# Scores in longer runs from tile 10, one transpose moved to a DMA, five stores moved to ScalarE's queue, and new latencies for the planner

## The chip, the cores and the metric

The kernel runs on one core of one Trainium2 chip. The metric is the device time of one execution in microseconds; of several executions the median is taken. A profile of one execution gives the times of single instructions, counted from the start of its span.

## The reference

Attention with a window, followed by a two-layer network on every token:

```python
B, H, S, D = 4, 8, 768, 64                  # q, k, v
keep = (pos_k < 8) | (0 <= pos_q - pos_k < 96)
bias = -slope[h] * dist                     # dist = |q - k|, and 96 for global keys outside the window
a    = softmax(where(keep, q @ k.T / 8 + bias, -1e9))
x    = (a @ v) as (3072 tokens, 512)        # heads side by side
h    = x @ w_in                             # 512 x 2048
out  = (h - tanh(h)) @ w_out                # 2048 x 512, float32
```

## The kernel before

**Tiles.** The 3072 tokens are 24 tiles of 128 rows, six per batch. Tiles are worked in the order `SEQ`: first the four tiles that begin a batch (numbers 0 to 3 below), then the other twenty in order (4 to 23). "Tile 10" here is always a place in that order. Since the window is shorter than a tile, a tile needs the keys of itself (block 0) and of the tile before it (block 1). The 8 global keys are copied into the first places of the previous tile's keys (`a_K`) and values (`a_V`).

**One tile's way.** POOL issues the loads of k, q and v, which cast to bf16 on their way (L237, L243; tiles 0 and 1 load k and q plainly from SP and ACT). k and q are transposed, for tiles 0 to 5 on TensorE (L278, L282, copied out of PSUM in L297), from `PE_T = 6` on by a DMA transpose that SP issues (`a_DT`, L286, into `qk`). The scores of a block (`a_S`, L315) are eight matmuls of 64 rows each, two heads at a time side by side in the array. ScalarE takes the exponential (`a_E`, L324), VectorE multiplies by a mask that holds bias and window (`a_M`, L330), TensorE multiplies by v with a column of ones beside it (`a_AV`, L343 and L347), VectorE divides by the sum (`a_R`, L355 and L356) and leaves `x`. x is transposed, for tiles below `PE_X = 9` on TensorE (`a_X`, L370, copied in L379), else by a DMA transpose on SP's queue (`a_DX`, L382).

**The network.** Tiles 0 to 5 go through it one by one, later ones in pairs. The first matmul (`m1`, L411) gives h in PSUM, with a moving operand of 128 columns for a single tile and 256 for a pair. ScalarE takes tanh (L423), VectorE subtracts (L430) and leaves `g`, the second matmul (`m2`, L445, 512 columns) sums over 16 pieces. The result is copied out of PSUM by ScalarE or VectorE (`m2_e`, L455) and stored (`store`, L460).

**Score runs.** Several blocks' scores can follow each other on TensorE as one run. From tile 4 a run holds the two blocks of one tile; from tile `R3 = 12` on, blocks are put into runs of `RUN = 3`, across tiles. A run holds two of the eight PSUM banks for each of its blocks.

**The order of work.** The program's order is fixed when it is built. `plan()` (from L658) plays the work through with a cost in microseconds for each step, takes at each point the step that can start first, and so writes the order of every engine; on the chip each engine then runs its own list in order, with semaphores between engines. The planner has a small model of DMA: each transfer has an amount of work (`T_ROWS, T_LD, T_W, T_ST, T_DT, T_DX`, L474), queues share the DMA engines by `SHARE`, at some times nothing moves (`FETCHES`, L473), and a transfer's semaphore comes a `TAIL` and a `slack` after its work. A DMA transpose begins, by this model, a fixed time after its issue, longer when loads of POOL are in flight (L713). Scores of a tile are held back until the network's matmuls have come within `AHEAD = 4.5` tiles of it.

**Stores.** `BY_POOL = 21` sends the stores of tiles 0 to 20 through POOL's queue, those of 21 and 22 through ScalarE's, and the three pieces of the last tile through SP's. POOL's queue also issues all loads, the last of them near 136 us.

The lines that the change touches and those that call on them:

Of the kernel before, what the change touches and what calls it, by code (L numbers as in the profile page):

```python
# [15 lines left out]
def kernel(  # L16
# [33 lines left out]
    APART = 4  # L50
    SEQ = [b * NQ for b in range(B)] + [t for t in range(NU) if t % NQ]
    pos = {t: u for u, t in enumerate(SEQ)}
    R3, RUN = 12, 3
    prev_of = {u: pos[t - 1] for u, t in enumerate(SEQ) if t % NQ}
    head_of = {u: pos[t - t % NQ] for u, t in enumerate(SEQ)}
    PLAIN = 2
    PE_T, PE_X = 6, 9
    HT, LAG, NG = 2, 2.0, 4
    SPLIT = (2, 2, 2)
    TJ = 4  # L60
# [400 lines left out]


    AHEAD, AHEAD_T = 4.5, 5.5
    BY_POOL, BY_SP = 21, 0
    YIELD = 0.0
    HALVES = 99
    EB = 2
# [2 lines left out]
    SLACK_DT, SLACK_DX = 1.0, 1.0  # L470
    WARM = (1.1, 7.0)
    COLD = 6.3
    FETCHES = [(15.8, 0.9), (23.0, 0.2), (31.0, 0.3)] + [(a, 0.9) for a in (40, 49, 61, 72, 83, 94, 105, 116, 127, 140)]  # L473
    T_ROWS, T_LD, T_W, T_ST, T_DT, T_DX = 0.67, 0.89, 1.3, 0.65, 1.05, 0.55  # L474
    RING = 5.8
    TAIL = {POOL: 0.45, SP: 0.8, ACT: 0.8}
    SHARE = {
# [180 lines left out]
    def plan():  # L658
# [24 lines left out]
        def fly(jobs, t, t_end):  # L683
            fin = {}
            while t < t_end:
                stop = [(a, n) for a, n in FETCHES if t < a + n][:1] or [(INF, 0)]
                if stop[0][0] <= t:
                    t = min(sum(stop[0]), t_end)
                    continue
                heads = [q for q in jobs if jobs[q] and jobs[q][0][1] <= t]  # L690
                later = min([jobs[q][0][1] for q in jobs if jobs[q] and jobs[q][0][1] > t] + [t_end])
                if not heads:
                    t = later
                    continue
                rate = SHARE[tuple(q in heads for q in (POOL, SP, ACT))]
                rate = {q: r for q, r in zip((POOL, SP, ACT), rate)}
                dt = min([later - t] + [jobs[q][0][2] / rate[q] for q in heads])
                dt = min(dt, stop[0][0] - t)
                t += dt
                for q in heads:  # L700
                    jobs[q][0][2] -= dt * rate[q]
                    if jobs[q][0][2] < 1e-6:
                        key = jobs[q].pop(0)[0]
                        fin[key] = t + TAIL[q] + ops[key]["slack"]
            return fin

        def fly_from(q, key, t, end):
            busy = flying[POOL]
            done.update(fly(flying, at_dma[0], t))
            at_dma[0] = max(at_dma[0], t)  # L710
            begin = end + (2.0 if q is POOL else 1.0)
            if key[0] in ("T", "Xe"):
                begin = t + (4.2 if busy else 2.2)  # L713
            if q is POOL:
                begin = max(begin, RING)
            flying[q].append([key, begin, ops[key]["dma"], q])
            landed[q].append(key)
            done.update(fly({k: [list(j) for j in v] for k, v in flying.items()}, at_dma[0], INF))
# [3 lines left out]
        def due_at(key):  # L722
            if flies[key] or key not in since:
                since[key] = max(
                    [0.0] + [start[a[1]] if a[0] == "issue" else done[a] for a in ops[key]["after"]]
                )
            return since[key]

        def at_of(x):
            return done[x] if isinstance(x, tuple) else x  # L730
# [18 lines left out]
        while ready or any(queues.values()):  # L749
# [16 lines left out]
            for key, n in cand:  # L766
# [4 lines left out]
                t = free[eng]  # L771
                if o["dma"] and len(landed[eng]) >= 8:
                    t = max(t, done[landed[eng][-8]])
                t = max(t, due_at(key))
# [4 lines left out]
                if o["hold"]:  # L779
# [3 lines left out]
                    t = max(t, w)  # L783
                for p in set(o["take"]):
                    n_p = o["take"].count(p)
                    if len(avail[p]) < n_p:
                        t = None
                        break
                    t = max(t, sorted(at_of(x) for x in avail[p])[n_p - 1])
# [7 lines left out]
            _, key, t, eng = best  # L797
# [7 lines left out]
            if o["at"]:  # L805
                done[key] = o["at"]
            elif o["dma"]:
                fly_from(o["eng"], key, t, end)
            else:
                done[key] = end + LAT[o["eng"]]  # L810
# [95 lines left out]
```

## Time and profile before

| what | value |
|---|---|
| median of 6 runs | 212.7 us (212.47 to 212.98) |
| the profiled execution's own time | 212.47 us |
| its span, first to last instruction | 210.7 us |
| granted TensorE clock, mean | 0.997 |
| TensorE's busy time | 205.6 us, 98% of the span |
| VectorE, ScalarE, POOL | 130.5, 118.7, 84.0 us |
| DMA transposes of k and q (18) | issue to landing 3.3 / 5.1 / 8.6 us (least, median, most) |
| DMA transposes of x (15) | 2.4 / 3.4 / 7.7 us |
| stores from POOL (21) | 0.58 us of POOL each, 2.3 to 6.6 us to landing |

A matmul's time in the profile is from its issue to its result, and matmuls follow each other before that, so the mean of one is longer than its share of the engine; the pieces of the chain of work that ended last show what each group took of the engine. The span leaves out what lies before the first and after the last instruction, 1.8 us in this execution.

### The profile page before, as it was taken

How to read it: one execution, taken by the hardware profiler on the slowest of the kernel's cores; microseconds unless marked ns; L12 is line 12 of the kernel's file. 1: busy time of each engine (PE TensorE's matmuls, PEld its weight loads, DVE VectorE, ACT ScalarE, POOL GpSimd, SP SyncE). 2: the span in 40 equal slices, each digit the busy share in tenths (PEclk: the TensorE clock that was granted, in tenths of full speed). 3: DMA queues.
4: the chain of work that ended last, by engine and by line, in shares of the span. 5: the costliest groups of instructions: out<-in, count | busy, mean ns of one | idle time of the engine just before them, and what ended most of it. 6: DMA issues, size and time to landing. Idle time of an engine off the chain costs nothing.

```text
span 210.7 us, 5364 instructions
## 1 busy us (share of the span) xinstructions
PE 205.6 (98%) x2198; PEld 145.2 (69%) x2198; DVE 130.5 (62%) x271; ACT 118.7 (56%) x182; POOL 84.0 (40%) x113
## 2 busy tenths in 40 slices
PE   7899999999999999999999999999999999999993
PEld 2669976876657758656957686668667676666663
DVE  6569865835767878465957595648548494434311
ACT  4767846535575685376648574848466763344420
POOL 8995685619548266466054520910110110111000
PEclk9999999999999999999999999999999999999998
DMA  5999999999999999999989995993510121110012
GB/s 178 185 188 177 189 192 181 189 149 141 248 178 185 160 153 152 136 159 204 129 157 145 124 194 109 112 157 82 123 55 20 60 49 52 53 50 18 37 50 100
DMA packets 104729, 27.49 MB, mean 130 GB/s; under 512 B 94656, under 2 KB 103104, under 8 KB 104704
## 3 DMA queue, kind: packets, MB, share of 16 engines
q0 software_dynamic: 75728, 18.62, 88.2%
q1 hardware_dynamic: 28144, 7.48, 23.9%
q10 hardware_dynamic: 832, 1.05, 1.5%
q8 instruction: 17, 0.28, 0.6%
q14 instruction: 8, 0.07, 0.1%
HBM read 27.26 MB, written 6.29 MB: 159 GB/s over the span
## 4 chain that ended last, share of the span: by engine, by line
PE 95%; DMA 2%; DVE 1%; ACT 0%; issue 0%; DVEq 0%
PE ps L411 41%; PE ps L445 40%; PE ps L315 6%; PE ps L343 3%; PE ps L347 2%; DMA kf<-in_k_dram 2%; PE ps L278 1%; PE ps L370 1%; PE ps L282 1%; PE ps L166 1%; DVE kh L297 0%; ACT qk L297 0%; DVE kq L256 0%; DVE ot L455 0%; DVEq L297 0%
## 5 line engine op out<-in xcount | busy, mean ns | idle before, releaser
L411 PE MATMUL ps<-xT,w_in_bf 128*128 128x256 bf16 (+1 forms) x960 | 96.3, 251 | 0.0
L445 PE MATMUL ps<-w_out_bf,g 128*128 128x512 bf16 (+3 forms) x416 | 93.3, 363 | 0.0
L411 PEld LDWEIGHTS <-w_in_bf 128*128 128x128 bf16 x960 | 77.2, 98 | 16.7
L423 ACT ACTIVATE th<-ps 128x512 f32<-128x512 f32 (+1 forms) x102 | 57.3, 574 | 53.5 <-PE ps L411 52.6
L430 DVE TENSOR_TENSOR g<-ps,th 128x512 bf16<-128x512 f32 (+1 forms) x102 | 64.3, 653 | 36.4 <-ACT th L423 35.8
L445 PEld LDWEIGHTS <-g 128*128 128x128 bf16 x416 | 38.3, 98 | 30.4
L460 POOL DMA_DIRECT2D out_dram<-ot x21 | 11.9, 568 | 90.4 <-ACT ot L455 87.4
L324 ACT ACTIVATE pd<-ps 128x1024 bf16<-128x1024 f32 x24 | 24.6, 1026 | 6.9 <-PE ps L315 6.9
L243 POOL DMA_DIRECT2D kq<-in_k_dram x20 | 18.0, 900 | 14.7 <-DMA qk<-kq 11.0
L324 ACT ACTIVATE po<-ps 128x1024 bf16<-128x1024 f32 x20 | 20.5, 1026 | 4.9 <-PE ps L315 4.9
L237 POOL DMA_DIRECT2D vb<-in_v_dram x24 | 21.8, 910 | 0.1
L455 ACT COPY ot<-ps 128x512 f32<-128x512 f32 x20 | 11.7, 586 | 12.0 <-PE ps L445 12.0
L330 DVE TENSOR_TENSOR po<-po,mk 128x1024 bf16<-128x1024 bf16 x20 | 13.8, 691 | 7.2 <-ACT po L324 7.2
L243 POOL DMA_DIRECT2D kq<-in_q_dram x20 | 18.0, 899 | 0.1
L356 DVE TENSOR_TENSOR x<-ps,rden 128x512 bf16<-128x512 f32 x24 | 16.6, 691 | 0.8
L330 DVE TENSOR_TENSOR pd<-pd,mk 128x1024 bf16<-128x1024 bf16 x20 | 13.8, 689 | 5.1 <-ACT pd L324 5.1
L343 PE MATMUL ps<-vb,pd 128*128 128x65 bf16 x192 | 14.1, 193 | 0.0
L343 PEld LDWEIGHTS <-pd 128*128 128x128 bf16 x192 | 12.5, 98 | 1.1 <-ACT pd L324 0.2
L347 PE MATMUL ps<-vb,po 128*128 128x65 bf16 x160 | 12.4, 193 | 0.0
L315 PEld LDWEIGHTS <-qk 64*128 64x128 bf16 x288 | 8.1, 94 | 5.3 <-issue 5.1
L315 PE MATMUL ps<-qk 64*128 64x128 bf16 x288 | 10.8, 217 | 0.0
L347 PEld LDWEIGHTS <-po 128*128 128x128 bf16 x160 | 10.4, 97 | 0.5
(49 smaller groups left out, 84.7 us busy)
## 6 DMA issues: line engine op xcount, KB each, us to landing
out_dram<-ot POOLq DMA_DIRECT2D x21, 256.0 KB, 3.2
vb<-in_v_dram POOLq DMA_DIRECT2D x24, 128.0 KB, 6.3
kq<-in_k_dram POOLq DMA_DIRECT2D x22, 128.0 KB, 5.9
kq<-in_q_dram POOLq DMA_DIRECT2D x22, 128.0 KB, 6.0
w_in_bf<-in_moe_w_in_dram POOLq DMA_DIRECT2D x8, 256.0 KB, 8.1
w_out_bf<-in_moe_w_out_dram POOLq DMA_DIRECT2D x8, 256.0 KB, 9.3
kf<-in_k_dram SPq DMA_DIRECT2D x2, 256.0 KB, 4.6
qf<-in_q_dram ACTq DMA_DIRECT2D x2, 256.0 KB, 3.9
```

The lines of the kernel that those rows point to most:

```text
L237: i = nc.gpsimd.dma_start(out=v_of(u)[:, :, 0:Dh], in_=by_head)
L243: i = nc.gpsimd.dma_start(out=dst.rearrange("p (h d) -> p h d", d=Dh), in_=by_head)
L315: nc.tensor.matmul(s[:, slot(2 * p + hh), :], kT(prev_of[u] if o else u)[r, p, :], qk[u][r, 0, p, :], start=u >= B, stop=True, skip_group_ ...
L324: nc.scalar.activation(pr[u, o].rearrange("q (a h) f -> q a h f", a=2)[:, part], sc[u, o][:, part, :].rearrange("q a (h f) -> q a h f", f= ...
L330: nc.vector.tensor_tensor(out=pr[u, o], in0=pr[u, o], in1=mk[:, :, mask_of(u, o) - 1, :], op=ALU.mult)
L343: nc.tensor.matmul(dst, pr[u, 0][:, slot(h), :], v_of(u)[:, h, :], start=True, stop=last,)
L347: nc.tensor.matmul(dst, pr[u, 1][:, slot(h), :], v_of(prev_of[u])[:, h, :], start=False, stop=True,)
L356: nc.vector.tensor_tensor(out=xs[u].rearrange("q (a h) d -> q a h d", a=2), in0=t[:, :, :, 0:Dh], in1=rden.to_broadcast([P, 2, H // 2, Dh] ...
L411: nc.tensor.matmul(t[:, (f - f0) * n : (f - f0 + 1) * n], w_in_bf[j][:, c, fo : fo + P], xT[b][:, c, o : o + n], start=(c == 0), stop=(c = ...
L423: nc.scalar.activation(h_view(ths[g, f0], g, m), h_view(hs[g, f0], g, m), AF.Tanh, bias=0.0, scale=1.0)
L430: nc.vector.tensor_tensor(out=gs[b][:, f0 : f0 + m, o : o + n], in0=h_view(hs.pop((g, f0)), g, m), in1=h_view(ths.pop((g, f0)), g, m), op= ...
L445: nc.tensor.matmul(os_[u, part][:, 0 : hi - lo], gs[b][:, f, t * P : (t + 1) * P], w_out_bf[f // FJ][:, f % FJ, lo:hi], start=(f == 0), st ...
```

## The change

Five edits. From tile 10 instead of 12, score blocks go in runs of three. x of tile 8 is transposed by a DMA on SP's queue instead of TensorE, so tile 8 is the first of its kind. Stores of tiles 16 to 20 are issued by ScalarE instead of POOL. In the planner, the times in which no DMA moves are cut (0.9 us to 0.4, and 0.2 and 0.3 to 0.1), three amounts of DMA work are lowered by 0.01 us, and a DMA transpose is taken to begin 3.4 us after its issue instead of 4.2 when loads are in flight, and 2.0 instead of 2.2 when none are. The last three alter no instruction themselves; they alter the order that the planner writes.

```diff
-    R3, RUN = 12, 3
+    R3, RUN = 10, 3
...
-    PE_T, PE_X = 6, 9
+    PE_T, PE_X = 6, 8
...
-    BY_POOL, BY_SP = 21, 0
+    BY_POOL, BY_SP = 16, 0
...
-    FETCHES = [(15.8, 0.9), (23.0, 0.2), (31.0, 0.3)] + [(a, 0.9) for a in (40, 49, 61, 72, 83, 94, 105, 116, 127, 140)]
-    T_ROWS, T_LD, T_W, T_ST, T_DT, T_DX = 0.67, 0.89, 1.3, 0.65, 1.05, 0.55
+    FETCHES = [(15.8, 0.9), (23.0, 0.1), (31.0, 0.1)] + [(a, 0.4) for a in (40, 49, 61, 72, 83, 94, 105, 116, 127, 140)]
+    T_ROWS, T_LD, T_W, T_ST, T_DT, T_DX = 0.66, 0.88, 1.29, 0.65, 1.05, 0.55
...
             if key[0] in ("T", "Xe"):
-                begin = t + (4.2 if busy else 2.2)
+                begin = t + (3.4 if busy else 2.0)
```

## The prediction

> **What bounds the kernel now.** I read the page's head and its fourth part first, then the stretches of 20 us, then the chain piece by piece, and last the stretches around single DMA transposes. The head and the chain:
>
> ```profile
> span 210.7 us, 5364 instructions
> PE 205.6 (98%) x2198; PEld 145.2 (69%) x2198; DVE 130.5 (62%) x271; ACT 118.7 (56%) x182; POOL 84.0 (40%) x113
> PE 95%; DMA 2%; DVE 1%; ACT 0%; issue 0%; DVEq 0%
> ```
>
> TensorE is busy for 98% of the span and makes 95% of the chain. Busy matmuls overlap, so I check this against the stretches (columns: stretch, sum, PE, PEld, DVE, ACT, POOL, clock, DMA share, GB/s):
>
> ```profile
> 20.00:40.00 20.00, 20.00 (x317) 16.67 (x315) 14.52 (x32) 12.30 (x22) 14.83 (x20) 1.00 1.60 191
> 40.00:60.00 20.00, 20.00 (x235) 13.17 (x232) 12.18 (x22) 9.68 (x14) 10.93 (x14) 1.00 1.80 172
> 60.00:80.00 20.00, 20.00 (x235) 13.97 (x230) 15.48 (x31) 14.30 (x20) 9.07 (x11) 1.00 1.82 171
> ```
>
> No idle time, full clock. The chain's pieces show that PE is not only covered but fed: 16 m2 matmuls of 512 columns take 3.45 to 3.56 us, or 216 to 222 ns each, as everywhere else. The waits of PE sum to 1.7 us in the whole run, all before 16 us. So only two things can move the end: the sum of PE's work, and a new wait of PE.
>
> **What the Trainium skill says.** "TensorE: Matmul & The Clock Gate", section "Wait — 56ns, not 53.3ns?", gives 55.6 ns for a warm 128-column matmul; the trace agrees, four transposes take 0.22 us. "DMA: Bandwidth & Descriptors", section "Issuing engines are not separate DMA queues", says that DMAs issued from ScalarE, SyncE and GpSimd share the same 16 engines and interleave, and that another issuer only saves sequencer time. The trace agrees: a store costs 0.54 to 0.60 us on POOL and 0.35 on ACT's queue, and landings stretch under load (the same DMA transpose takes 3.3 to 8.6 us). Section "Queues, rings and completion order" of that page has each engine round-robin between the rows with work; so a transpose issued amid loads waits for packets of loads, which fits that spread.
>
> **The PE sum.** x of tile 8 leaves PE: four transposes.
>
> ```profile
> 64.97 0.55 PE ps L315 x16
> 65.52 0.33 PE ps L370 x4
> 118.35 0.78 PE ps L315 x24
> ```
>
> Elsewhere in the chain the same four take 0.22 us; the 0.33 here has the changeover after a score run in it, which whatever follows pays. So 0.22 to 0.23 us go. The copy behind them (0.58 us on ACT or 0.42 on DVE) goes too, worth nothing, since neither engine holds PE.
>
> The score runs look like a gain and are none. Before: blocks of tiles 4 to 11 in 8 runs of two, tiles 12 to 23 in 8 runs of three, with the first four tiles 20 runs. After, counted in the built program: 6 runs of two, 9 of three, one of a single block, again 20. A run pays about 0.10 us when it begins and 0.095 when it ends (L315's start-to-start steps beside its neighbours); 16 matmuls take 0.55 us and 24 take 0.78, 0.23 per block either way. Zero.
>
> PE's other matmuls are the same number (2198 less 4). Sum: -0.23 us.
>
> **New waits: DMA transposes.** The fitted figures make the planner believe that a transpose lands 0.8 us sooner when loads are in flight and 0.2 sooner otherwise, so it sets the score runs earlier. PE's order is unchanged for the first 370 matmuls (to 28.5 us), SP's and POOL's to 56 us. I take each transpose's margin in the trace and subtract the PE work that the built program no longer puts ahead of its reader. Tile 6 (columns: start, us, what):
>
> ```profile
> 37.54 1.33 SPq L286 DMA_TRANSPOSE qk<-kq  x1
> DMA to landing us min/median/max: 8.3/8.3/8.3
> 47.97 0.62 PE L315 MATMUL ps<-qk 64*128 64x128 bf16 x16
> ```
>
> It lands at 45.9 and is read at 47.97: margin 2.1. In the new order 32 m1 matmuls of 128 columns (56 ns each, 1.8 us) stand behind this run instead of ahead. Left: 0.3 us. Tile 9:
>
> ```profile
> 53.18 1.65 SPq L286 DMA_TRANSPOSE qk<-kq  x1
> DMA to landing us min/median/max: 8.6/8.6/8.6
> 64.90 0.40 PE L315 MATMUL ps<-qk 64*128 64x128 bf16 x8
> ```
>
> Landed 61.8, margin 3.1; 8 m2 (1.73 us) and 8 m1 of 256 columns (0.88) move behind it: 0.5 left. Tile 7: 5.6 - 1.8 = 3.8. Tile 8: 4.6 - 1.7 = 2.9. Tile 11: 5.5 - 2.8 = 2.7. Tile 14: 7.15 - 4.6 = 2.6. x of tiles 12 and 13: 3.5 - 1.7 = 1.8. The rest keep more. Weights: the sixth piece of w_out landed at 39.6, was read at 41.3, and its reader moves up by 1.1: 0.6 left; the seventh and eighth keep over 2.
>
> So with the landings of the trace nothing waits, but the cushion falls from 2.1 us to 0.3 at one place and to 0.5 at another. A wait of PE is lost time in full: PE runs in order and is full up to the end, so the tanh, g and m2 behind it are all late by as much. Once PE has slipped at tile 6 the later margins grow by the slip; delays don't add.
>
> **The other parts.** Tile 8's x on SP: one DMA transpose more, 1.19 us of the queue, 2.4 to 7.7 to landing. x of tile 8 was written at 65.06, and the matmuls that lead to it move up by 1.7, so SP has it from 63.3 and is done with it near 64.5. Behind it on SP stands tile 11's k/q transpose, issued at 64.59 in the trace when its loads had landed: up to 0.6 later (1.2 if x comes late), of the 2.7 us left. Behind that, tile 9's x and tile 12's k/q with 2.7 and 4.8. Its own readers, the m1 of tiles 8 and 9, waited for tile 9's x anyway (landed 75.27, read 79.27, moved up 1.3: 2.7 left). POOL's next loads wait for k/q transposes, so they shift by the same tenths; tile 14 has 2.6 for it. Cost zero; with that cover gone, 1.2 us once.
>
> Runs of three at tiles 10 and 11: six of eight PSUM banks held while three exps follow on ACT (0.92 us apart). Eight such runs in the trace cost PE nothing. Here they fall into the stretch where DVE has 15.5 and ACT 14.3 busy of 20 us, the fullest. Bound: nothing, or one exp (0.92) at each of one or two of the places. I take nothing.
>
> Stores of tiles 16 to 20: five issues of 0.35 us onto ACT, ahead of the next tanh. From 160 us ACT is busy 11.2 and then 8.4 of 20 us, with gaps of about 1.1 us before a tanh; hidden. If all showed, 1.75 us. POOL loses five stores after its last load (137 us), nothing waits for them. The last tile's stores stay on SP, so the tail from the last matmul (207.3) to the end stays about 3.4 us.
>
> **Sum.** The profiled execution took 212.47 with its span of 210.7, 1.8 around it. Less 0.23: span 210.45, time 212.24. The six runs lie in two heaps, 212.47 to 212.53 and 212.87 to 212.98, and the profile is of the lower; the median, 212.7, less 0.23 is 212.47. I say 212.5.
>
> **Rivals.** A measurement of this kernel can tell about 0.2% (0.43 us) from no change.
> 1. No wait, or waits under 0.66 us in sum: 212.3 to 213.1. For it, the margins above, all positive. Chance 0.48.
> 2. Tile 6's or 9's k/q transpose lands late. For it: landings of equal transposes spread from 3.3 to 8.6 us, and the order of stores against loads on POOL changes from 56 us, inside tile 9's flight; against: until 46 us both queues issue the same in the same order. Landing x later than in the trace costs x - 0.3 (tile 6) or x - 0.5 (tile 9); with the 0.23 gained, it is slower by over 0.43 from x of 1 us. x = 1.3: 213.2 to 213.5; x = 2: 214.2. Chance 0.20.
> 3. ACT or DVE falls behind at the runs of three from tile 10: one or two exps, 0.9 to 1.8, so 213.4 to 214.3. Against it, the eight runs without cost. Chance 0.12.
> 4. The stores on ACT show: up to 1.75, 214.2. Chance 0.03.
> 5. Faster by over 0.43: the 0.23 with the upper heap's 0.4 us gone, 212.1. That needs the upper heap to come from a wait that the new order avoids; the profile is of the lower heap and shows none. Chance 0.17.
> That the change does nothing would be 212.7 and lies in case 1.
>
> **Numbers.** Faster 0.17, same 0.48, slower 0.35 (cases 2 to 4). The range leaves out the ends of cases 2 to 4 and 5: 212.0 to 214.2. Case 1's own: 212.3 to 213.1.
>
> **What would show it.** L370 with 32 matmuls instead of 36, SP with 16 x transposes, ACT with seven stores, 20 runs of L315; last matmul near 207.0; PE 20.00 in every stretch of 20 us from 20 to 200. Wrong: a wait of PE on the qk transposes near 46 or 62 us, idle PE between 60 and 80 with ACT or DVE as releaser, a gap before a tanh that follows a store on ACT, or a start before 16 us that is other than before.

## The result, and the profile after

The changed kernel takes 214.01 us (median of 18 executions, 212.4 to 216.9) against 212.62 (39 executions, 212.23 to 213.43) for the kernel before, taken in turn on the same chips. The ratio is 1.0059, with an interval of 1.0042 to 1.0076: slower by 0.6%. The ratios here and below leave out executions marked as slow (here the one of 216.9 us, with a mean clock of 0.992; below, one or two each in three experiments), so a ratio can be smaller than that of the medians beside it. The executions of the changed kernel lie 4.5 us apart, those before 1.2, so the loss is not a fixed amount. The forecast was 212.5 and no measurable change; 214.01 lies in its range of 212.0 to 214.2, but on the side of rivals 2 to 4, not of the case taken as likeliest.

The profiled execution took 214.11 us, 1.64 more than the profiled one of before: its span grew by 1.30 us, and what lies before the first and after the last instruction from 1.78 us to 2.13. The head of the profile's page of the changed kernel, and its chain:

```profile
span 212.0 us, 5354 instructions
PE 205.8 (97%) x2194; PEld 145.0 (68%) x2194; DVE 129.2 (61%) x264; ACT 122.2 (58%) x188; POOL 81.2 (38%) x108
PE 85%; DMA 11%; DVE 1%; ACT 1%; issue 1%; DVEq 0%
PE ps L411 37%; PE ps L445 35%; DMA qk<-kq 9%; PE ps L315 5%; PE ps L343 3%; PE ps L347 2%; DMA kf<-in_k_dram 2%; PE ps L278 1%; PE ps L282 1%; PE ps L370 1%; PE ps L166 1%; DVE kh L297 0%; DVE qk L335 0%; ACT qk L297 0%; ACT po L324 0%
```

TensorE has the 2194 matmuls that were counted and still leads, but DMA went from 2% of the chain to 11%, and 9% of that is one kind: the DMA transposes of k and q. The clock was full throughout this execution. The stretches of 20 us (columns as in the prediction: sum, PE, PEld, DVE, ACT, POOL, clock, DMA share, GB/s):

```profile
20.00:40.00 20.00, 20.00 (x314) 16.55 (x311) 13.88 (x29) 13.37 (x23) 15.15 (x20) 1.00 1.60 191
40.00:60.00 20.00, 18.53 (x230) 12.59 (x229) 13.08 (x24) 9.35 (x15) 7.43 (x11) 1.00 1.90 158
60.00:80.00 20.00, 19.89 (x218) 13.75 (x217) 13.82 (x27) 12.83 (x19) 12.11 (x15) 1.00 2.06 170
```

Before, all three held 20.00 of PE. Now 1.47 us are missing before 60 us. The waits of PE in the changed kernel (us in total, times, longest), and PE's timeline around the gap (start, us, what, and in brackets the idle time before it and what ended it):

```profile
PE ps L315 <- DMA qk<-kq: 1.5, 1, 1.5
```

```profile
56.90 1.03 PE L445 MATMUL ps<-w_out_bf,g 128*128 128x512 bf16 x4
59.39 0.62 PE L315 MATMUL ps<-qk 64*128 64x128 bf16 x16 [1.47 <-DMA qk<-kq]
```

This is the score run of tile 8: k and q of that tile were not yet transposed. A smaller wait of the same kind stands inside the first run of three that tile 11 takes part in. It shows on the queue of weight loads (PEld), since the sixteen weight loads of tile 10 in that run were through and its matmuls had begun:

```profile
75.30 0.23 PEld L315 LDWEIGHTS <-qk 64*128 64x128 bf16 x8 [0.28 <-DMA qk<-kq]
```

The first matmul of the run of tile 8 starts 1.53 us later than the usual changeover would have it; tile 9 loses 0.04 and tile 11 0.27. Sum 1.84; less the 0.23 us of PE work that went, 1.61. The last matmul starts at 208.90 instead of 207.27, 1.63 later. So the whole delay of PE in this execution is late transposes of k and q. (The 0.35 us outside the span are another matter; see the point on the tail at the end.)

How late, and beside what? Tile 8's transpose in the changed kernel, its issue on SP's queue and its way to landing, then the three stores (256 KB each) that POOL issued just after it:

```profile
48.08 1.24 SPq L286 DMA_TRANSPOSE qk<-kq  x1
DMA to landing us min/median/max: 11.3/11.3/11.3
L460 POOL DMA_DIRECT2D out_dram<-ot x3: 562/590/597, 48.4 to 49.5; - x3
DMA to landing us min/median/max: 9.6/9.6/9.7
```

And the same in the kernel before, the transpose first:

```profile
L286 SPq DMA_TRANSPOSE qk<-kq x1: 1233/1233/1233, 48.4 to 48.4; - x1
DMA to landing us min/median/max: 6.6/6.6/6.6
L460 POOL DMA_DIRECT2D out_dram<-ot x3: 545/592/599, 49.4 to 50.6; - x3
DMA to landing us min/median/max: 5.8/6.1/6.2
```

The transpose of the same 256 KB takes 11.3 us instead of 6.6, and the stores 9.6 instead of 6.1. The stores landed between 58.0 and 59.1 us, the transpose at 59.34, right behind them. Tile 7's transpose ahead of it on the queue took 7.1 us instead of 4.4, and in the trace the packets of tile 8's start about when tile 7's have landed: at 52.6 us with a landing at 52.78, before at 51.1 with a landing at 50.76. From that landing on, tile 8's took 6.6 us instead of 4.2. The stretches of 4 us show that the DMA engines moved less. Changed kernel first, then before; the last column is GB/s:

```profile
48.00:52.00 4.00, 4.00 (x60) 3.06 (x58) 3.36 (x8) 1.75 (x3) 2.04 (x4) 1.00 2.33 110
52.00:56.00 4.00, 4.00 (x56) 2.85 (x54) 2.62 (x6) 1.92 (x3) 2.65 (x3) 1.00 1.95 139
56.00:60.00 4.00, 2.53 (x39) 1.70 (x38) 2.49 (x4) 1.86 (x4) 0.16 (x2) 1.00 1.19 224
```

```profile
48.00:52.00 4.00, 4.00 (x45) 2.48 (x45) 2.66 (x5) 1.94 (x2) 3.81 (x6) 1.00 1.78 147
52.00:56.00 4.00, 4.00 (x60) 3.06 (x58) 3.09 (x6) 1.65 (x3) 2.01 (x3) 1.00 1.40 276
56.00:60.00 4.00, 4.00 (x52) 2.19 (x49) 2.27 (x4) 2.56 (x4) 3.22 (x4) 1.00 1.80 137
```

From 48 to 56 us the engines moved 4 x (110 + 139) = 996 KB, before 4 x (147 + 276) = 1692. With a higher busy share (2.33 against 1.78 in the first stretch) they moved less; what was outstanding then came after 56 us, at 224 GB/s. Tile 8's transpose belonged to it.

The shortfall is not even. From 49.5 to 50.5 us hardly anything moved: 3 and 9 GB/s in the two halves. In the experiment below with the stores back on POOL, which has the same order up to there, it is 2 and 9; in the five profiled executions that still have the old order there (the kernel before, the planner's figures undone, and each of the three visible parts alone) it is 138 to 215. A second such stretch lies from 55.5 to 56.5 us, with 35 and 38 GB/s against 285 and 124 before. Both fall into the flight of tile 8's transpose, so by estimate they make some 2 of the 4.7 us by which it is longer. The planner's list has a stop of this kind at 49 us, and the change cut it from 0.9 us to 0.4. What makes the engines stop isn't shown.

### The profile page after: what moved, and what is told of

It reads as the page before. It is cut to its first block, busy times and chain, and to the rows that moved or that the text cites. A ratio compares the mean times of both kernels' runs of the same rounds, so it can differ in the third digit from the quotient of the medians.

```text
span 212.0 us, 5354 instructions
## 1 busy us (share of the span) xinstructions
PE 205.8 (97%) x2194; PEld 145.0 (68%) x2194; DVE 129.2 (61%) x264; ACT 122.2 (58%) x188; POOL 81.2 (38%) x108
## 4 chain that ended last, share of the span: by engine, by line
PE 85%; DMA 11%; DVE 1%; ACT 1%; issue 1%; DVEq 0%
PE ps L411 37%; PE ps L445 35%; DMA qk<-kq 9%; PE ps L315 5%; PE ps L343 3%; PE ps L347 2%; DMA kf<-in_k_dram 2%; PE ps L278 1%; PE ps L282 1%; PE ps L370 1%; PE ps L166 1%; DVE kh L297 0%; DVE qk L335 0%; ACT qk L297 0%; ACT po L324 0%
## 5 line engine op out<-in xcount | busy, mean ns | idle before, releaser
L445 PE MATMUL ps<-w_out_bf,g 128*128 128x512 bf16 (+3 forms) x416 | 94.7, 363 | 0.0
L460 POOL DMA_DIRECT2D out_dram<-ot x16 | 9.2, 582 | 38.4 <-ACT ot L455 38.4
L455 ACT COPY ot<-ps 128x512 f32<-128x512 f32 x19 | 11.1, 585 | 8.8 <-PE ps L445 8.5
```

The source lines that it names most:

```text
L445: nc.tensor.matmul(os_[u, part][:, 0 : hi - lo], gs[b][:, f, t * P : (t + 1) * P], w_out_bf[f // FJ][:, f % FJ, lo:hi], start=(f == 0), st ...
```

## The experiments

The theory after the result: the planner's new figures set the score runs earlier and make loads, stores and transposes fall together in another way; a DMA transpose then lands after its run, and PE stands. Rivals: the runs of three press ScalarE or VectorE, the x transposes in SP's queue push the k/q transposes back, or the stores on ScalarE cost something. The measured ratios are to the kernel before, taken in the same turns.

### The planner's figures undone, the rest kept

```diff
-    FETCHES = [(15.8, 0.9), (23.0, 0.1), (31.0, 0.1)] + [(a, 0.4) for a in ...]
-    T_ROWS, T_LD, T_W, T_ST, T_DT, T_DX = 0.66, 0.88, 1.29, 0.65, 1.05, 0.55
+    FETCHES = [(15.8, 0.9), (23.0, 0.2), (31.0, 0.3)] + [(a, 0.9) for a in ...]
+    T_ROWS, T_LD, T_W, T_ST, T_DT, T_DX = 0.67, 0.89, 1.3, 0.65, 1.05, 0.55
...
-                begin = t + (3.4 if busy else 2.0)
+                begin = t + (4.2 if busy else 2.2)
```

> The changed kernel with all of the planner's figures as they were before (4.2 and 2.2 us to the begin of a DMA transpose, the old stops and amounts of work); runs of three from tile 10, tile 8's x by DMA and the stores on ScalarE's queue stay. Theory 'margins' (the planner's new figures set score runs before their transposes land): score runs of tiles 6 to 9 stand where they stood before, tile 11's 1.5 us later, so no wait on qk; four transposes less on TensorE: 212.3 to 212.6, no slower than before. Theory 'added DMA' (tile 8's x on SP, stores on ScalarE's queue, or runs of three make the waits): waits stay, 213.5 or more.

Measured: 212.74 us, ratio 1.0006 (0.9995 to 1.0017). No score run waits for a DMA. The last matmul starts at 207.05, 0.22 earlier than before (207.27): the sum of PE's work was right. With runs of three from tile 10, x of tile 8 by DMA and the stores on ScalarE all in place, the kernel is as fast as before. These three together cost nothing that can be told when planned with the old figures.

### The planner's figures alone

The edit is the reverse of the last, on the kernel before.

> The kernel before with the planner's new figures alone; x of tile 8 on TensorE, runs of three from tile 12, stores on POOL. Theory 'margins': tiles 6 to 9 move up by 1.7 to 2.6 us as in the changed kernel, tiles 10 and 11 by 4.4, so TensorE waits on qk near 46 to 76 us, with a wide spread: 213.3 to 215. Theory 'added DMA': no wait, 212.6.

Measured: 214.91 us, ratio 1.0076 (1.0044 to 1.0109). PE's timeline of this kernel, where most of the loss is:

```profile
71.76 1.03 PE L445 MATMUL ps<-w_out_bf,g 128*128 128x512 bf16 x4
74.39 0.62 PE L315 MATMUL ps<-qk 64*128 64x128 bf16 x16 [1.60 <-DMA qk<-kq]
```

That is tile 11 (landed 74.34). Tiles 6 and 10 were also read right at their landing and lost 0.16 and 0.19. So the figures alone are enough to make transposes late, and which tile is hit differs from the changed kernel. With the run before, this puts the loss on the planner's figures, and on no instruction that was added or removed.

### The stores back on POOL

```diff
-    BY_POOL, BY_SP = 16, 0
+    BY_POOL, BY_SP = 21, 0
```

> The changed kernel with the stores of tiles 16 to 20 back on POOL; TensorE's order is the same as in the changed kernel. Theory 'margins': same waits, 213.5 to 214.5. Theory 'stores on ScalarE': back at 212.5.

Measured: 214.21 us, ratio 1.0056 (1.0035 to 1.0076), as slow as the changed kernel. TensorE's order is the same as there, and ScalarE issues its first store at 164.9 us there, long after the waits. The waits of this kernel:

```profile
PE ps L315 <- DMA qk<-kq: 0.9, 2, 0.7
```

Here tile 8 landed at 58.16 and lost 0.25, tile 9 lost 0.77 and tile 11 0.15. Up to these places the program does not differ from the changed kernel, where it was 1.53, 0.04 and 0.27. The loss is much the same, but its place moves between executions of one order: a landing is not a fixed number.

### Thin stores: is it the stores' traffic?

In the changed kernel's order, tiles 0 to 7 store only 32 of their 512 columns; the rest of these tiles' output is left out. Nothing else is touched.

```diff
+        if u < 8:
+            hi = lo + 32
```

> The changed kernel in unchanged order, but of tiles 0 to 7 only 32 of 512 output columns are stored: the rest of those rows is left out. If the stores of the first tiles share the DMA engines with the k/q transposes and so make them land late, the transposes of tiles 7 to 9 land about 2 us sooner and the waits near 58 and 64 us go: 212.3 to 213. If the lateness comes from the loads alone, the waits stay: 213.5 to 214.5.

Measured: 212.76 us, ratio 1.0004 (0.9993 to 1.0016). Tile 8's transpose and PE's timeline at its run, in this kernel:

```profile
DMA to landing us min/median/max: 7.1/7.1/7.1
...
57.16 1.03 PE L445 MATMUL ps<-w_out_bf,g 128*128 128x512 bf16 x4
58.12 0.62 PE L315 MATMUL ps<-qk 64*128 64x128 bf16 x16
```

The transpose lands at 55.69, 2.4 us ahead of its reader, and tile 9's takes 4.8 us instead of 10.0. All waits on `qk` are gone with the order unchanged. So it takes the stores' traffic to make the transposes late; their place behind one another in SP's queue and the reader's place are unchanged and don't do it alone. This agrees with what the Trainium skill states in "DMA: Bandwidth & Descriptors", section "Queues, rings and completion order": an engine takes turns between the rows that have work, so a transpose shares with whatever else is outstanding. Whether bytes or the number of packets decide was not tried. Nor is it separated how much the stores do by sharing and how much by the stop near 49.5 us, which is shorter here: 65 and 247 GB/s in the two halves from 49.5 to 50.5.

### Which of the figures

Only the begin of a transpose restored to 4.2 and 2.2:

```diff
-                begin = t + (3.4 if busy else 2.0)
+                begin = t + (4.2 if busy else 2.2)
```

> The changed kernel with only the begin of a DMA transpose back at 4.2 and 2.2 us; the shorter stops stay. In the built order the score runs stand against those of the kernel before: tile 6 up by 1.8 us, tiles 7 to 9 by 0.9 each, tile 11 by 2.0. Theory 'margins': between the two, waits at tiles 6 to 9 in part of the executions, 212.7 to 213.7. Theory 'the begin alone does it': 212.4 to 212.6.

Measured: 213.79 us, ratio 1.0051 (1.0036 to 1.0065). The waits for transposes are gone, with 1.7 us of margin at tile 6, 3.1 at tile 8 and 1.9 at tile 9. But this order has waits of another kind:

```profile
PE ps L315 <- DVE x L356: 1.0, 1, 1.0
...
PE ps L411 <- DVE rden L355: 0.5, 1, 0.5
```

A score run waits for VectorE's divide to free its PSUM. In the profiled execution the loss has another cause, these 1.5 us of waits and a later start (tile 4's run begins at 23.22 instead of 22.79 us). The run says that the shorter begin is needed for the late transposes, not that restoring it is enough.

Only the times in which nothing moves, and the amounts of work, restored (the first four lines of the first diff):

> The changed kernel with only the stops and the amounts of DMA work as before; the begin of a DMA transpose stays at 3.4 and 2.0. Tile 6 where it stood before, tiles 7 and 8 up by 0.9, tile 9 as before. Theory 'margins': hardly a wait, 212.4 to 213.0. Theory 'the begin alone does it': waits stay, 213.5 or more.

Measured: 212.35 us, ratio 0.9988 (0.9976 to 1.0000), with no wait on `qk`; 2.8 us of margin at tile 8 and 2.5 at tile 9, though the begin stays short. So in the profiled executions each half undone takes the late transposes away; it is both together that bring the runs too close. This is the fastest version with all of the visible parts of the change, at the edge of what can be told from no change.

### More slack instead

The planner adds a slack to each transpose of k and q; it goes from 1 us to 4, all else as in the changed kernel:

```diff
-    SLACK_DT, SLACK_DX = 1.0, 1.0
+    SLACK_DT, SLACK_DX = 4.0, 1.0
```

> The changed kernel with 4.0 instead of 1.0 us of slack for the landing of a k/q transpose in the planner, all else as changed. Score runs of tiles 6, 7, 9 and 10 stand 0.8 to 3.5 us later than in the kernel before. Theory 'margins': no wait on qk, spread as narrow as before, 212.2 to 212.6. Theory 'added DMA' (the x transpose and the stores on ScalarE's queue slow landings for good): 213 or more.

Measured: 212.76 us, ratio 1.0001 (0.9985 to 1.0017). Every transpose of k and q lands at least 2 us ahead of its reader. The new figures do no harm once runs keep a distance; two waits for VectorE of 0.2 us each appear, which is about the 0.22 that should have been gained.

### Two x transposes by DMA

On the kernel before, x of tiles 7 and 8 by DMA, with slack of 2 us:

```diff
-    PE_T, PE_X = 6, 9
+    PE_T, PE_X = 6, 7
...
-    SLACK_DT, SLACK_DX = 1.0, 1.0
+    SLACK_DT, SLACK_DX = 2.0, 2.0
```

> A try at a faster version: the kernel before with x of tiles 7 and 8 by DMA and 2.0 us of slack for both kinds of transpose in the planner, all else as before. Eight transposes less on TensorE, 0.45 us. Score runs of tiles 7 to 9 later than before, tile 10 up by 3.1 of a margin of 6.8. Theory 'margins': 212.1 to 212.4. If the added transposes push landings back by more than 3 us: 213 or more.

Measured: 217.24 us, ratio 1.0205 (1.0172 to 1.0238), a miss in size and in cause. The waits of PE, and the stretch in which they lie:

```profile
PE ps L343 <- DVE pd L330: 1.7, 1, 1.7
...
PE ps L411 <- DMA xT<-x: 0.7, 1, 0.7
PE ps L347 <- DVE po L330: 0.7, 1, 0.7
```

```profile
60.00:80.00 20.00, 16.81 (x181) 11.65 (x180) 11.87 (x22) 11.62 (x17) 12.00 (x15) 0.91 1.89 162
```

PE lacks 3.2 us here, and the granted clock is 0.91 in this stretch, where the next four stretches have 1.00; so beside the 3.1 us of waits, PE's work was slower too. The trace's clock record has 0.50 from 70.87 to 74.28 us and 1.00 around it. PE's timeline has it right after the third wait:

```profile
71.16 5.16 PE L411 MATMUL ps<-xT,w_in_bf 128*128 128x256 bf16 x32 [0.74 <-DMA xT<-x]
```

Eight such matmuls take 0.87 us elsewhere (70.89 to 71.76 in the kernel with the planner's figures alone), 32 of them 3.5; here they take 5.2. All six executions of this kernel have a mean clock of 0.992, so it is not a chance of one. That the two x transposes do it by themselves isn't shown, since the order changed with the slack as well.

### One part alone, on the kernel before

Stores of tiles 16 to 20 on ScalarE's queue:

```diff
-    BY_POOL, BY_SP = 21, 0
+    BY_POOL, BY_SP = 16, 0
```

> The kernel before with the stores of tiles 16 to 20 on ScalarE's queue and nothing else; the order of TensorE is that of the kernel before. All theories that put the loss on the planner's figures: 212.5, no difference, no wait of TensorE. If a store on ScalarE's queue holds a tanh up: up to 1.75 us more.

Measured: 212.39 us, ratio 0.9989 (0.9977 to 1.0001). PE's order is that of before and the last matmul starts at the same 207.27, but the span is 210.3 instead of 210.7. The end is shorter. At the end of the program SP waits for the semaphores of the DMAs one by one, in a list whose order is the same in all traces here. SP's waits of this kind by stretches (count, durations in ns, first and last start), and the drain after them, in before:

```profile
L901 SPq EVENT_SEMAPHORE  x2: 28/28/28, 209.4 to 209.5; - x2
...
L901 SPq EVENT_SEMAPHORE  x6: 28/28/28, 209.5 to 209.8; - x6
L901 SPq DRAIN  x2: 7/10/13, 209.9 to 209.9; - x2
```

And in this kernel:

```profile
L901 SPq EVENT_SEMAPHORE  x6: 27/28/28, 208.3 to 208.6; - x6
...
L901 SPq EVENT_SEMAPHORE  x2: 28/28/28, 209.4 to 209.4; - x2
L901 SPq DRAIN  x1: 13/13/13, 209.5 to 209.5; - x1
```

In both, the last store lands at about 209.4. Before, it signals a semaphore (102) that is third in the list, so seven waits of about 0.06 us each follow; with the stores moved, it signals another (117), next to last, two such waits follow, and most of the list has been walked by 208.6. So the five moved DMAs changed which semaphore the last one gets. From the last matmul to the end of the span it is 3.06 us here and 3.42 before, 0.36 less, which the prediction did not have: five waits less make 0.31 of it, and the last store landed 0.05 sooner.

x of tile 8 by DMA, alone:

```diff
-    PE_T, PE_X = 6, 9
+    PE_T, PE_X = 6, 8
```

> The kernel before with x of tile 8 by DMA alone. Theory 'sum of TensorE' (only the four transposes and the landings count; no score run moves up by more than 2.8 us of 7.1): 212.2 to 212.4. Theory 'new list' (every new plan is a new order, and where the planner's costs of VectorE are below the trace's, as 0.61 for a mask product that takes 0.69, TensorE waits on VectorE): 1 to 2 us more, with VectorE as releaser between 60 and 130 us, as in the run with the begin undone.

Measured: 214.05 us, ratio 1.0068 (1.0047 to 1.0089): the sum of TensorE missed, and the theory 'new list' was right in size and in releaser. PE's timeline of this kernel:

```profile
94.05 0.23 PE L315 MATMUL ps<-qk 64*128 64x128 bf16 x1
95.75 0.60 PE L315 MATMUL ps<-qk 64*128 64x128 bf16 x15 [1.47 <-DVE g L430]
```

and VectorE's work just before:

```profile
94.40 0.69 DVE L356 TENSOR_TENSOR x<-ps,rden 128x512 bf16<-128x512 f32 x1
95.01 0.68 DVE L430 TENSOR_TENSOR g<-ps,th 128x512 bf16<-128x512 f32 x1
```

No transpose is late. The new order puts a score run into PSUM that a subtraction of VectorE still reads, and puts a divide ahead of that subtraction. The planner counts a subtraction at about 0.60 us and a mask product at 0.61; the trace has 0.68 and 0.69. That these small errors led the planner to this order is argued; no run with corrected costs was made.

Runs of three from tile 10, alone:

```diff
-    R3, RUN = 12, 3
+    R3, RUN = 10, 3
```

> The kernel before with runs of three from tile 10 alone. Same number of runs, same matmuls. Theory 'sum of TensorE': 212.5. Theory 'new list': 212.6 to 213.2 with VectorE as releaser; theory 'margins' has no wait on qk here, since tiles 6 to 9 stand where they stood and tiles 10 and 11 stand later.

Measured: 212.93 us, ratio 1.0008 (0.9993 to 1.0022); no wait on `qk`, last matmul at 207.34. To within what can be told, the runs of three are the zero that was counted.

### A version with the stops undone and some slack

On the changed kernel: the stops and amounts as before (the same lines as in "Which of the figures"), and a slack of 1.5 us for k/q transposes and 2.0 for those of x.

```diff
-    SLACK_DT, SLACK_DX = 1.0, 1.0
+    SLACK_DT, SLACK_DX = 1.5, 2.0
```

> A try at a faster version: the changed kernel with the stops and amounts of before and, in the planner, 1.5 us of slack for k/q and 2.0 for x transposes. Tiles 6 to 11 stand against the kernel before at 0, up 0.9, and then 0.5 to 4.1 us later; x of tiles 10 and 11 1.8 later. Theory 'margins' with 'new list': no wait on a transpose, at most 0.2 us on VectorE, four transposes less: 212.2 to 212.5, with the spread of the kernel before.

Measured: 213.36 us, ratio 1.0025 (1.0012 to 1.0038), a miss. The waits list only work at the start:

```profile
PE ps L393 <- DVE zero L865: 1.0, 1, 1.0
PE ps L282 <- DMA kq<-in_k_dram: 0.3, 1, 0.3
```

Work also begins later: tile 4's run starts at 23.38 us instead of 22.79, which with the 0.22 us saved puts the last matmul at 207.64. The span ends 4.1 us after it, where the changed kernel and five others with these stores on ScalarE have 3.03 to 3.09 (the planner's figures undone, 3.71, is the second exception). The traces show where: the last store landed 2.57 us after its issue, against 1.51 in the run with more slack, where it was issued at the same 208.28 us; with the planner's figures undone the last two took 2.39 and 2.14. Why these stores took longer is open, and whether the other executions of this kernel did the same isn't on record. No version beats the kernel before by more than can be told.

## Why the prediction was wrong, point by point

**The PE sum, -0.23 us.** Right: 0.22 in the profiled execution where the order is planned with the old figures. The zero for the runs of three held when tried alone.

**Moved readers.** Right as to the order. Tile 8's run was to move up by 1.7 us from 59.58; without its wait it would have begun at 59.39 - 1.53 = 57.86, which is 1.72.

**"With the landings of the trace nothing waits."** This is the step that failed. It took landings from one execution of another order and subtracted only the reader's move. Tile 8 was credited with 2.9 us left; its landing moved from 54.95 to 59.34, by 4.4, so 1.5 were missing: the wait that was measured. Tiles 6 and 9, called the tightest, kept 1.39 and nearly nothing (0.04 lost). The change moves the loads and stores as well as the readers, and the thin stores show that the stores' traffic decides whether the landing comes in time. Part of the 4.4 is the spread of one order: the kernel before, the planner's figures undone and the three visible parts alone have the same order on PE, POOL and SP until after this landing, and there it comes at 54.95, 55.96, 55.95, 56.72 and 57.07. The trace that the margin was taken from has the earliest of the five. The other 2.3 us, from 57.07 to 59.34, lie outside that spread; with the stores back on POOL, a second execution of the new order, it is 58.16, also later than all five. The prediction had the evidence: equal transposes from 3.3 to 8.6 us, and "a transpose issued amid loads waits for packets of loads". A margin of 2.9 us against a spread of 5 us was no margin, and rival 2 held that spread only against the two tightest tiles.

**"SP's and POOL's order is unchanged to 56 us."** Unchanged order did not mean unchanged overlap. Tile 7's transpose was issued at 45.66 instead of 46.36 and the three stores at 48.36 instead of 49.43, so they met other traffic. How much of the stretch from 6.6 to 11.3 us comes from this shift alone was not separated; two stretches of about 1 us in which almost nothing moved lie in it, and in none of the five executions of the old order did the first of them occur.

**Rivals.** Rival 2 is right in kind, with 0.20, and in the size that it gave (213.2 to 214.2), but it named tiles 6 and 9. Rivals 3 and 4 did not act in this kernel; rival 3's mechanism, VectorE late at a score run, shows in two experiments (the begin restored, x alone), though not with runs of three alone.

**"Cost zero" for the stores and the x transpose.** Right for the stores on ScalarE. Of the x transpose alone the run shows a loss of 0.7%, by VectorE in the order that was written for it and not by SP's queue; with the runs and the stores beside it and the old figures, none.

**"The tail stays about 3.4 us."** Wrong by about 0.35 us in the kernel's favour, by the semaphore list. The span grew by 1.3 us only, while the last matmul is 1.63 later. In the time nothing of it is left, since the sum also took the 1.8 us around the span as fixed: they were 2.1 to 2.2 in all 19 executions of the changed kernel, 1.7 to 1.8 in those of the kernel before. The stores back on POOL and the thin stores, which share the changed order, have 2.1 to 2.2 as well, the begin undone 1.9 to 2.1, and all other versions 1.7 to 1.9. The thin stores have them without a late transpose, and the planner's figures alone have late transposes without them. So these 0.35 us, about a quarter of the loss, go with the order that the planner wrote and not with late transposes; why is open. In the runs of the stores alone the shorter end is not offset, and the ratio there is 0.9989.

**"Delays don't add."** Not so in kind: tile 11 lost 0.27 after tile 8's 1.53. POOL's next loads wait for the transposes (31.0 us in 12 waits, before 11.0 in 4), so a late transpose starts the next tile's loads late.

## What to carry to other kernels

A DMA's landing depended here on the traffic around it: when a change re-orders loads and stores, hold each margin against the spread of equal transfers in the trace, not against the one landing there. A plan with shorter latencies removes the distance that absorbed the spread of landings; take the mean for the latency, then keep the spread as slack. And where a planner writes the whole order, parts tried one by one are new orders and don't add up, so read in every run which wait was the cause before giving the difference to the edit.

## What was not expected of the hardware

- The DMA transpose of the same 256 KB took 3.1 to 11.3 us from issue to landing over these runs; three stores of 256 KB outstanding beside it went with 11.3, three of 16 KB with 7.1.
- The program's end depends on which semaphore the last DMA signals: the waits in SP's list take about 0.06 us each, and seven of them after the last landing's own, or two, made 0.31 us of a difference of 0.36.
- The DMA engines can almost stand for about 1 us: 3 and 9 GB/s in the halves from 49.5 to 50.5 us in the changed kernel, 2 and 9 in a second execution of its order, 138 to 215 in five executions of the old one.
- What lies outside the span is not the same for every version of one kernel: 2.1 to 2.2 us with the changed order, 1.7 to 1.8 before.
- With x of tiles 7 and 8 by DMA the clock was halved (0.50) from 70.87 to 74.28 us. In the 3.7 us before that, from 67.19 on, PE worked 0.84 us in two pieces between waits of 1.7, 0.7 and 0.7. With the single wait of 1.5 us in the changed kernel the clock stayed at 1.00. The Trainium skill, "TensorE: Matmul & The Clock Gate", section "Part 1: The HAM clock gate (the "warmup" mystery)", has the clock fall to half after an idle window of about 3.4 us; the trace agrees on the half, but no single wait here was longer than 1.7. How much work within such a window would keep the clock up was not tried.
